# Gated linear attention followed by an MLP: from one head at a time through DRAM to one chunk of all heads at a time, interleaved with the MLP

## The chip, the core and the metric

The kernel runs on one core of one Trainium2 chip. The metric is device time in microseconds (us) of one launch, taken as the median of several runs. A core has five engines that run side by side, each in the order of its own instructions: TensorE (PE, matrix products and transposes; its weight loads are listed apart as PEld), VectorE (DVE), ScalarE (ACT, functions such as Exp, Ln and Silu, each from a table that has to be loaded), GpSimd (POOL) and SyncE (SP, which here only issues DMAs). Sixteen DMA engines move data between DRAM and on-chip memory; SP and POOL each have a queue of transfers that all sixteen serve. PE writes its results to PSUM, from where another engine has to fetch them.

## The reference

Attention has 4 batches, 8 heads, 768 steps and a head width of 48. Each head keeps a 48x48 state that decays by a gate per row and step. The MLP runs over the 3072 x 384 result, with a hidden width of 2048.

```
f = 1.0 / (1.0 + np.exp(-f_logit))
for t in range(S):
    state = f[:, :, t, :, None] * state + np.einsum('bhd,bhe->bhde', k[:, :, t], v[:, :, t])
    y[:, :, t] = np.einsum('bhd,bhde->bhe', q[:, :, t], state)
x = y.transpose(0, 2, 1, 3).reshape(B * S, H * D)
h = x @ w_in
out = (h * (1.0 / (1.0 + np.exp(-h)))) @ w_out
```

Both kernels use the chunked form of this: within a chunk of 128 steps, with `a` the running product of the gates, y is the lower triangle of (q·a)(k/a)ᵀ times v, plus (q·a) times the state before the chunk.

## The kernel before

**Attention** (L59 to L115) loops over the 4 batches, the 8 heads of each and the 6 chunks of each head: 192 passes. A head's four inputs are loaded by POOL with a cast to bf16 (L64 to L72) and its log gates are made by Sigmoid and Ln on ACT. A pass sums the log gates (`cs_ps`, L80), transposes q and k on PE (L82, L84), takes `a` = Exp (L86), `ia` by DVE's reciprocal (L88), makes `qg`, `ki` and `kb` on DVE (L91 to L95), transposes `kb` back (L97, L99), forms and masks the scores (`at_ps`, `atm`, L101, L103), the output (`y_ps`, L105, L106) and the next state (`d_ps`, `new_state`, L108, L110). The output, 128 rows of 48 floats, goes to a DRAM tensor called `bridge` (L115). Matmuls have 48 rows, or 48 columns, on one side or the other.

**The MLP** comes after that. Both weights are loaded by POOL (L120, L122) once attention's pools are closed. The 24 blocks of 128 tokens are read back from `bridge` (L140) and transposed on PE into `xT` (L143, L144). Then `h_ps` (L151) and Silu (L153) run over 16 blocks of the hidden width and 6 blocks of 512 tokens, and last `o_ps` (L158), its copy (L161) and the output (L162).

A scheduler in the framework sets each engine's order in this kernel: the loads of a next head, for example, stand ahead of the current one's passes, bounded by the two buffers of pool `hb`.

Of the kernel before, what the change touches and what calls it, by code (L numbers as in the profile page):

```python
# [10 lines left out]
F32 = mybir.dt.float32  # L11
BF16 = mybir.dt.bfloat16
AF = mybir.ActivationFunctionType
ALU = mybir.AluOpType


@with_exitstack
def kernel(
    ctx: ExitStack,
    tc: tile.TileContext,  # L20
    q: bass.AP,
    k: bass.AP,
    v: bass.AP,
    f_logit: bass.AP,
    moe_w_in: bass.AP,
    moe_w_out: bass.AP,
    out: bass.AP,
):
# [16 lines left out]
    maskU = singles.tile([C, C], F32)  # L45
    make_upper_triangular(nc, maskU, 1.0, diag=True)
    ident = singles.tile([C, C], BF16)
    make_identity(nc, ident)

    attn_ctx = ExitStack()  # L50
    sb = attn_ctx.enter_context(tc.tile_pool(name="sb", bufs=3))
    hb = attn_ctx.enter_context(tc.tile_pool(name="hb", bufs=2))
    ps = attn_ctx.enter_context(tc.tile_pool(name="ps", bufs=1, space=bass.MemoryType.PSUM))
    ps2 = attn_ctx.enter_context(tc.tile_pool(name="ps2", bufs=1, space=bass.MemoryType.PSUM))
    psA = attn_ctx.enter_context(tc.tile_pool(name="psA", bufs=1, space=bass.MemoryType.PSUM))
    psY = attn_ctx.enter_context(tc.tile_pool(name="psY", bufs=2, space=bass.MemoryType.PSUM))
    stp = attn_ctx.enter_context(tc.tile_pool(name="stp", bufs=2))

    for b in range(B):  # L59
        for h in range(H):  # L60
            state = stp.tile([D, D], BF16)
            nc.vector.memset(state, 0.0)
            logf_all = hb.tile([C, NCH, D], BF16)
            nc.gpsimd.dma_start(out=logf_all, in_=f_logit[b, h].rearrange("(c ci) d -> ci c d", ci=C))  # L64
            nc.scalar.activation(logf_all, logf_all, AF.Sigmoid)
            nc.scalar.activation(logf_all, logf_all, AF.Ln)  # L66
            q_all = hb.tile([C, NCH, D], BF16)
            nc.gpsimd.dma_start(out=q_all, in_=q[b, h].rearrange("(c ci) d -> ci c d", ci=C))
            k_all = hb.tile([C, NCH, D], BF16)
            nc.gpsimd.dma_start(out=k_all, in_=k[b, h].rearrange("(c ci) d -> ci c d", ci=C))  # L70
            v_all = hb.tile([C, NCH, D], BF16)
            nc.gpsimd.dma_start(out=v_all, in_=v[b, h].rearrange("(c ci) d -> ci c d", ci=C))  # L72
            for c in range(NCH):
                s0 = c * C
                logf_cd = logf_all[:, c, :]
                q_cd = q_all[:, c, :]
                k_cd = k_all[:, c, :]
                v_cd = v_all[:, c, :]
                cs_ps = ps.tile([D, C], F32)
                nc.tensor.matmul(cs_ps, logf_cd, triu)  # L80
                qT_ps = ps2.tile([D, C], BF16)
                nc.tensor.transpose(qT_ps, q_cd, ident)  # L82
                kT_ps = ps2.tile([D, C], BF16)
                nc.tensor.transpose(kT_ps, k_cd, ident)  # L84
                a = sb.tile([D, C], F32)
                nc.scalar.activation(a, cs_ps, AF.Exp)  # L86
                ia = sb.tile([D, C], F32)
                nc.vector.reciprocal(ia, a)  # L88
                cs_last = a[:, C - 1:C]
                qg = sb.tile([D, C], BF16)  # L90
                nc.vector.tensor_mul(qg, qT_ps, a)  # L91
                ki = sb.tile([D, C], BF16)
                nc.vector.tensor_mul(ki, kT_ps, ia)  # L93
                kb = sb.tile([D, C], BF16)
                nc.vector.tensor_scalar(kb, ki, cs_last, None, ALU.mult)  # L95
                kbT_ps = ps.tile([C, D], BF16)
                nc.tensor.transpose(kbT_ps, kb, ident[:D, :D])  # L97
                kbT = sb.tile([C, D], BF16)
                nc.scalar.copy(kbT, kbT_ps)  # L99
                at_ps = psA.tile([C, C], F32)  # L100
                nc.tensor.matmul(at_ps, ki, qg)  # L101
                atm = sb.tile([C, C], BF16)
                nc.vector.tensor_mul(atm, at_ps, maskU)  # L103
                y_ps = psY.tile([C, D], F32)
                nc.tensor.matmul(y_ps, atm, v_cd, start=True, stop=False)  # L105
                nc.tensor.matmul(y_ps, qg, state, start=False, stop=True)  # L106
                d_ps = ps.tile([D, D], F32)
                nc.tensor.matmul(d_ps, kbT, v_cd)  # L108
                new_state = stp.tile([D, D], BF16)
                nc.vector.scalar_tensor_tensor(new_state, state, cs_last, d_ps,  # L110
                                               ALU.mult, ALU.add)
                state = new_state
                y_sb = sb.tile([C, D], F32)
                nc.scalar.copy(y_sb, y_ps)  # L114
                nc.sync.dma_start(out=bridge[b * S + s0:b * S + s0 + C, h * D:h * D + D], in_=y_sb)  # L115
# [8 lines left out]
    MT = 512
    n_mt = NT // MT
    n_kt = d_model // 128
    n_nt = d_ff // 128
    n_dt = d_model // 128

    xpool = ctx.enter_context(tc.tile_pool(name="xpool", bufs=1))  # L130
    hpool = ctx.enter_context(tc.tile_pool(name="hpool", bufs=1))
    ptp = ctx.enter_context(tc.tile_pool(name="ptp", bufs=2, space=bass.MemoryType.PSUM))
    php = ctx.enter_context(tc.tile_pool(name="php", bufs=4, space=bass.MemoryType.PSUM))
    pop = ctx.enter_context(tc.tile_pool(name="pop", bufs=2, space=bass.MemoryType.PSUM))
    opool = ctx.enter_context(tc.tile_pool(name="opool", bufs=3))

    xT = xpool.tile([128, n_kt, NT], BF16)
    for mi in range(NT // 128):
        x_sb = opool.tile([128, d_model], BF16)
        nc.gpsimd.dma_start(out=x_sb, in_=bridge[mi * 128:(mi + 1) * 128, :])  # L140
        for ki in range(n_kt):
            xt_ps = ptp.tile([128, 128], BF16)
            nc.tensor.transpose(xt_ps, x_sb[:, ki * 128:(ki + 1) * 128], ident)  # L143
            nc.vector.tensor_copy(xT[:, ki, mi * 128:(mi + 1) * 128], xt_ps)  # L144

    hT = hpool.tile([128, n_nt, NT], BF16)
    for ni in range(n_nt):
        for mi in range(n_mt):
            h_ps = php.tile([128, MT], F32)
            for ki in range(n_kt):  # L150
                nc.tensor.matmul(h_ps, w_in_sb[:, ki, ni * 128:(ni + 1) * 128], xT[:, ki, mi * MT:(mi + 1) * MT],  # L151
                                 start=(ki == 0), stop=(ki == n_kt - 1))
            nc.scalar.activation(hT[:, ni, mi * MT:(mi + 1) * MT], h_ps, AF.Silu)  # L153

    for mi in range(NT // 128):
        o_ps = pop.tile([128, d_model], F32)
        for ni in range(n_nt):
            nc.tensor.matmul(o_ps, hT[:, ni, mi * 128:(mi + 1) * 128], w_out_sb[:, ni, :],  # L158
                             start=(ni == 0), stop=(ni == n_nt - 1))
        o_sb = opool.tile([128, d_model], F32)  # L160
        nc.vector.tensor_copy(o_sb, o_ps)  # L161
        nc.sync.dma_start(out=out[mi * 128:(mi + 1) * 128, :], in_=o_sb)  # L162


# [28 lines left out]
```

## Time and profile before

| what | value |
|---|---|
| median of 3 runs | 632.35 us (632.18 to 632.67) |
| profiled execution: its span, first to last instruction | 630.9 us |
| ACT_TABLE_LOAD at L86, L65, L66 | 61 + 32 + 32, 1.283 us each |
| first `h_ps` of the dense MLP (timeline) | 504.27 us |
| bytes read from and written to DRAM | 29.88 MB, 9.44 MB |

The page of a profile names groups of instructions by line, engine and operation, with what goes out of and into them, the count, the busy time and the mean ns of one; behind the second bar stands how long the engine was idle just before them, and what ended that. Slices are fortieths of the span, with the busy share in tenths.

### The profile page before, as it was taken

The numbers are of one execution on the slowest core, as the hardware profiler recorded it, in microseconds if no ns is written. First come the engines' busy times: TensorE is split into PE (matmuls) and PEld (weight loads), VectorE is DVE, ScalarE is ACT, GpSimd is POOL, SyncE is SP. The second block draws the span as 40 slices with busy tenths as digits, with TensorE's granted clock in tenths as the row PEclk, the third lists the DMA queues.
The fourth block names the chain that finished last, engine by engine and source line by source line (L and its number), as shares of the span: only waits on it lengthen the run. The fifth ranks groups of instructions, "written<-read, shape, count | busy, mean of one in ns | idle before, by whom it ended". The sixth has DMA issues, their size and how long they took to land.

```text
span 630.9 us, 8131 instructions
## 1 busy us (share of the span) xinstructions
PE 438.1 (69%) x2273; PEld 226.0 (36%) x2280; DVE 388.9 (62%) x1280; ACT 359.1 (57%) x862; POOL 121.4 (19%) x164
## 2 busy tenths in 40 slices
PE   1666666666666666676666666666724699999997
PEld 0333333333333333333333333333311244446664
DVE  1888887777888877888888778888822400002221
ACT  6666777656667777666677776666301189970000
POOL 5222222322222322222223222222032300000000
PEclk9999999999999999999999999999999999999999
DMA  7444445545444454544444545444088500002222
GB/s 37 30 32 29 35 32 36 50 30 35 31 31 34 30 40 29 35 31 31 32 32 32 37 30 34 30 32 30 14 141 128 66 0 1 0 1 76 75 76 76
DMA packets 137422, 24.93 MB, mean 40 GB/s; under 512 B 128800, under 2 KB 136992, under 8 KB 137376
## 3 DMA queue, kind: packets, MB, share of 16 engines
q0 software_dynamic: 106272, 14.95, 35.0%
q1 hardware_dynamic: 31104, 9.45, 6.2%
q8 instruction: 18, 0.29, 0.2%
q14 instruction: 28, 0.23, 0.1%
HBM read 29.88 MB, written 9.44 MB: 62 GB/s over the span
## 4 chain that ended last, share of the span: by engine, by line
PE 29%; issue 28%; DVE 20%; ACT 11%; DMA 6%; POOL 6%; POOLq 0%; ACTq 0%; DVEq 0%
DVE ia L88 11%; PE o_ps L158 10%; PE h_ps L151 10%; DMA x_sb<-bridge 5%; ACT L66 4%; DVE new_state L110 3%; ACT a L86 3%; ACT L86 2%; DVE kb L95 2%; PE y_ps L105 2%; PE kbT_ps L97 2%; PE cs_ps L80 2%; DVE atm L103 2%; PE y_ps L106 1%; POOL logf_all L64 1%
## 5 line engine op out<-in xcount | busy, mean ns | idle before, releaser
L88 DVE RECIPROCAL ia<-a 48x128 f32<-48x128 f32 x192 | 180.0, 938 | 39.9 <-ACT a L86 39.9
L99 ACT COPY kbT<-kbT_ps 128x48 bf16<-128x48 bf16 x192 | 37.1, 193 | 85.8 <-PE kbT_ps L97 85.5
L80 PE MATMUL cs_ps<-triu,logf_all 128*48 128x128 bf16 x192 | 51.3, 267 | 46.9 <-ACT a L86 46.8
L82 PE MATMUL qT_ps<-ident,q_all 128*48 128x128 bf16 x192 | 54.4, 283 | 42.1 <-DVE qg L91 36.1
L161 DVE COPY o_sb<-o_ps 128x384 f32<-128x384 f32 x24 | 13.4, 558 | 109.5 <-PE o_ps L158 109.5
L86 ACT ACT_TABLE_LOAD x61 | 78.3, 1283 | 1.1
L153 ACT ACTIVATE hT<-h_ps 128x512 bf16<-128x512 f32 x96 | 57.3, 597 | 32.8 <-PE h_ps L151 28.4
L108 PE MATMUL d_ps<-v_all,kbT 128*48 128x48 bf16 x192 | 44.9, 234 | 42.2 <-ACT kbT L99 42.1
L151 PE MATMUL h_ps<-xT,w_in_sb 128*128 128x512 bf16 x281 | 67.6, 398 | 9.0 <-DMA w_in_sb<-in_moe_w_in_dram 8.8
L86 ACT ACTIVATE a<-cs_ps 48x128 f32<-48x128 f32 x192 | 52.1, 271 | 37.9 <-DVE new_state L110 27.7
L158 PE MATMUL o_ps<-w_out_sb,hT 128*128 128x384 bf16 x384 | 63.0, 327 | 6.2 <-DMA w_out_sb<-in_moe_w_out_dram 6.2
L110 DVE SCALAR_TENSOR_TENSOR new_state<-new_state,a,d_ps 48x48 bf16<-48x48 bf16 x160 | 37.9, 237 | 41.3 <-PE d_ps L108 41.3
L97 PE MATMUL kbT_ps<-ident,kb 48*128 48x48 bf16 x192 | 41.9, 218 | 29.5 <-DVE atm L103 18.6
L103 DVE TENSOR_TENSOR atm<-at_ps,maskU 128x128 bf16<-128x128 f32 x192 | 56.2, 293 | 6.0 <-PE at_ps L101 1.7
L84 PE MATMUL kT_ps<-ident,k_all 128*48 128x128 bf16 x192 | 57.6, 300 | 0.5 <-DMA k_all<-in_k_dram 0.5
L101 PE MATMUL at_ps<-qg,ki 48*128 48x128 bf16 x192 | 54.6, 284 | 0.0
L64 POOL DMA_DIRECT2D logf_all<-in_f_logit_dram x32 | 26.4, 826 | 145.7 <-PE at_ps L101 124.5
L91 DVE TENSOR_TENSOR qg<-qT_ps,a 48x128 bf16<-48x128 bf16 x192 | 52.8, 275 | 0.0
L93 DVE TENSOR_TENSOR ki<-kT_ps,ia 48x128 bf16<-48x128 bf16 x192 | 52.6, 274 | 0.0
L95 DVE TENSOR_SCALAR kb<-ki,a 48x128 bf16<-48x128 bf16 x192 | 52.1, 271 | 0.1
L114 ACT COPY y_sb<-y_ps 128x48 f32<-128x48 f32 x192 | 37.0, 193 | 25.4 <-PE y_ps L106 24.1
L158 PEld LDWEIGHTS <-hT 128*128 128x128 bf16 x384 | 37.6, 98 | 31.8 <-issue 4.1
(38 smaller groups left out, 537.2 us busy)
## 6 DMA issues: line engine op xcount, KB each, us to landing
bridge<-y_sb SPq DMA_DIRECT2D x192, 24.0 KB, 1.7
out_dram<-o_sb SPq DMA_DIRECT2D x24, 192.0 KB, 1.9
logf_all<-in_f_logit_dram POOLq DMA_DIRECT2D x32, 72.0 KB, 2.9
q_all<-in_q_dram POOLq DMA_DIRECT2D x32, 72.0 KB, 3.0
k_all<-in_k_dram POOLq DMA_DIRECT2D x32, 72.0 KB, 3.2
v_all<-in_v_dram POOLq DMA_DIRECT2D x32, 72.0 KB, 2.9
x_sb<-bridge POOLq DMA_DIRECT2D x24, 96.0 KB, 2.6
w_in_sb<-in_moe_w_in_dram POOLq DMA_DIRECT2D x1, 1536.0 KB, 10.9
```

The lines of the kernel that those rows point to most:

```text
L80: nc.tensor.matmul(cs_ps, logf_cd, triu)
L84: nc.tensor.transpose(kT_ps, k_cd, ident)
L86: nc.scalar.activation(a, cs_ps, AF.Exp)
L88: nc.vector.reciprocal(ia, a)
L95: nc.vector.tensor_scalar(kb, ki, cs_last, None, ALU.mult)
L97: nc.tensor.transpose(kbT_ps, kb, ident[:D, :D])
L101: nc.tensor.matmul(at_ps, ki, qg)
L103: nc.vector.tensor_mul(atm, at_ps, maskU)
L110: nc.vector.scalar_tensor_tensor(new_state, state, cs_last, d_ps, ALU.mult, ALU.add)
L151: nc.tensor.matmul(h_ps, w_in_sb[:, ki, ni * 128:(ni + 1) * 128], xT[:, ki, mi * MT:(mi + 1) * MT], start=(ki == 0), stop=(ki == n_kt - 1))
L153: nc.scalar.activation(hT[:, ni, mi * MT:(mi + 1) * MT], h_ps, AF.Silu)
L158: nc.tensor.matmul(o_ps, hT[:, ni, mi * 128:(mi + 1) * 128], w_out_sb[:, ni, :], start=(ni == 0), stop=(ni == n_nt - 1))
```

## The change

The kernel is rewritten around chunks. A **group** g is one chunk of 128 steps of all 4 batches and 8 heads: 512 tokens. There are 6 groups, and for each of them:

- `load(g)` (SP): the four inputs in f32, one DMA each, of 128 steps by 32 heads in pieces of 48 floats; two buffers.
- `prep(g)`: `e` = Exp(−f) and `lf` = Ln(1 + e), two ACTIVATEs of 1536 elements a row; v is cast into `vp`, in which zeros stand around each head; then for each batch the running sums `cs` (one matmul of 384 columns), `a` and `ia` by two Exp, `qg` on DVE and `ki` on POOL. `al` is the decay over the whole chunk, by 16 matmuls of one column. Heads lie 64 elements apart, so that two make 128 rows.
- `attend(g)`: for each batch 8 transposes of head pairs and one copy `qk`; 8 score matmuls and two masked products `atm`; the outputs `y_ps`, which come out transposed (384 features by 128 tokens) and are copied to `xT`, the operand of the MLP; and the state `st`, held in SBUF with zero blocks for the other heads.
- `mlp_in(g)` and `mlp_out(g)`: the same MLP, on the 512 tokens of the group. Both weights are loaded at the start (POOL, behind six memsets of 2048 elements a row).

The order is written out by hand. `interleave` takes parts from its streams, by the numbers that they yield, so that each gets through at the same rate. After `prep(0)`, attend(0) runs with prep(1); then iteration g has mlp_in(g) with the first half of attend(g + 1), and mlp_out(g) with its second half and prep(g + 2). Transposes run one batch ahead of scores and two ahead of outputs. `bridge`, its reads and the 72 transposes of x are gone, and so is the reciprocal.

```diff
-    bridge = nc.dram_tensor("bridge", (NT, HD), F32, kind="Internal").ap()
...
+    acc = ctx.enter_context(tc.tile_pool(name="acc", bufs=3, space=PSUM))
+    tps = ctx.enter_context(tc.tile_pool(name="tps", bufs=1, space=PSUM))
+    aps = ctx.enter_context(tc.tile_pool(name="aps", bufs=1, space=PSUM))
+    hps = ctx.enter_context(tc.tile_pool(name="hps", bufs=2, space=PSUM))
...
+    def load(g):
+        tiles = {}
+        for name, src in (("f", f_logit), ("k", k), ("q", q), ("v", v)):
+            t = ld.tile([C, B, H, D], F32, name=f"{name}_ld", tag=f"{name}_ld")
+            nc.sync.dma_start(out=t.rearrange("p b h d -> p (b h) d"), in_=group_view(src, g))
...
+    def prep(g):
...
+        nc.scalar.activation(e, t["f"], AF.Exp, scale=-1.0)
+        nc.scalar.activation(lf[i][:, :, :, 0:D], e, AF.Ln, bias=1.0)
+        for b in range(B):
+            nc.gpsimd.tensor_copy(
+                vp[i][:, b, 128:].rearrange("p (h w) -> p h w", w=VW)[:, :, 0:D], t["v"][:, b])
+        yield 0.0
+        for b in range(B):
+            cs = acc.tile([C, H, D], F32, name="cs", tag="acc")
+            nc.tensor.matmul(cs, triu, lf[i][:, b, :, 0:D], start=True, stop=True)
+            a = wk.tile([C, H, D], F32, name="a")
+            nc.scalar.activation(a, cs, AF.Exp, scale=-1.0)
+            ia = wk.tile([C, H, D], F32, name="ia")
+            nc.scalar.activation(ia, cs, AF.Exp, scale=1.0)
+            nc.vector.tensor_mul(qg[i][:, b, :, 0:D], t["q"][:, b], a)
+            nc.gpsimd.tensor_mul(ki[i][:, b, :, 0:D], t["k"][:, b], ia)
+            yield 162.0
+        al_ps = acc.tile([C, B, NP], F32, name="al_ps", tag="acc")
+        for b in range(B):
+            for p in range(NP):
+                nc.tensor.matmul(al_ps[:, b, p:p + 1], lf[i][:, b, 2 * p:2 * p + 2, :], ones,
...
+        def transposes(b):
...
+            sb = wk.tile([128, 2, NP, C], BF16, name="qk")
+            nc.vector.tensor_copy(sb, t_ps)
...
+        def outputs(b):
...
+                for n, (l, r) in enumerate(terms):
+                    nc.tensor.matmul(y_ps[:, t, :], l, r, start=(n == 0), stop=(n == len(terms) - 1))
+            nc.vector.tensor_copy(x[:, :, b, :], y_ps)
...
+        for s in range(B + 2):
+            if s < B:
+                order.append((transposes, s, 560.0))
+            if 1 <= s <= B:
+                order.append((scores, s - 1, 450.0))
+            if s >= 2:
+                order.append((outputs, s - 2, 1100.0))
+                if g < NCH - 1:
+                    order.append((state, s - 2, 450.0))
...
+    with tc.manual_schedule():
+        for _ in prep(0):
+            pass
+        interleave((attend(0), ATT), (prep(1), PREP))
+        for g in range(NCH):
+            if g + 2 < NCH:
+                load(g + 2)
...
+            first = [(mlp_in(g), 16 * 650.0)]
+            if att is not None:
+                first.append((half(att, ATT / 2), ATT / 2))
+            interleave(*first)
+            second = [(mlp_out(g), 16 * 650.0)]
+            if att is not None:
+                second.append((att, ATT / 2))
+            if g + 2 < NCH:
+                second.append((prep(g + 2), PREP))
+            interleave(*second)
```

**The middle of an iteration, ACT.** Before, ACT's rows in attention mix a head's gate functions with the Exp and the copies of each pass (`kbT` and `y_sb` are copies of PE's results).

```order
L65 ACT_TABLE_LOAD
L65 ACTIVATE logf_all<-logf_all 128x288
L114 COPY y_sb<-y_ps 128x48
L86 ACT_TABLE_LOAD
L86 ACTIVATE a<-cs_ps 48x128
```

Of the change, the same engine from the end of prep(1) through mlp_in(0) (L243, Silu) into prep(2):

```order
L150 ACTIVATE al<-al_ps 128x16
L243 ACT_TABLE_LOAD
L243 ACTIVATE hT<-h_ps 128x512 x16
L127 ACT_TABLE_LOAD
L127 ACTIVATE e<-f_ld 128x1536
L128 ACT_TABLE_LOAD
L128 ACTIVATE lf_105<-e 128x32x48
L137 ACT_TABLE_LOAD
L137 ACTIVATE a<-cs 128x384
L139 ACTIVATE ia<-cs 128x384
```

The gate functions of a group now stand in one place, behind all 16 Silu of the iteration.

**The same place, PE.** Before, PE's rows at a pass's start and the pass's rest go through single heads:

```order
L80 LDWEIGHTS logf_all
L80 MATMUL cs_ps<-triu,logf_all 48x128
L105 LDWEIGHTS atm
L105 MATMUL y_ps<-v_all,atm 128x48
L106 LDWEIGHTS qg
L106 MATMUL y_ps<-new_state,qg 128x48
```

Of the change, where the second half of iteration 0 has begun (L198 is the last of batch 1's outputs, L250 mlp_out; four `o_ps` stand ahead of the outputs):

```order
L198 LDWEIGHTS vp_112
L198 MATMUL y_ps<-atm,vp_112 128x128
L135 LDWEIGHTS triu
L135 MATMUL cs<-lf_105,triu 128x384
L250 LDWEIGHTS hT
L250 MATMUL o_ps<-w_out_sb,hT 128x384
```

`cs`, which reads what ACT's Ln writes, stands ahead of all but four of the 64 `o_ps`.

**The start, DVE.** Before, DVE's rows are a chain for one pass after another:

```order
L88 RECIPROCAL ia<-a 48x128
L91 TENSOR_TENSOR qg<-qT_ps,a 48x128
L93 TENSOR_TENSOR ki<-kT_ps,ia 48x128
L88 RECIPROCAL ia<-a 48x128
L95 TENSOR_SCALAR kb<-ki,a 48x128
L103 TENSOR_TENSOR atm<-at_ps,maskU 128x128
```

Of the change, from prep(0) (`qg_107`) into attend(0), with `qg_108` of prep(1) between its steps:

```order
L140 TENSOR_TENSOR qg_107<-q_ld,a 128x8x48 x4
L171 COPY qk<-t_ps 128x1024
L140 TENSOR_TENSOR qg_108<-q_ld,a 128x8x48
L171 COPY qk<-t_ps 128x1024
L183 TENSOR_TENSOR atm<-a_ps,triu 128x512 x2
L140 TENSOR_TENSOR qg_108<-q_ld,a 128x8x48
```

A product of group 1, which reads `q_ld` of load(1), now stands ahead of most of attend(0).

More of the change, by code (lines that the diff above doesn't have):

```diff
@@ L55 @@
-    psA = attn_ctx.enter_context(tc.tile_pool(name="psA", bufs=1, space=bass.MemoryType.PSUM))
-    psY = attn_ctx.enter_context(tc.tile_pool(name="psY", bufs=2, space=bass.MemoryType.PSUM))
-    stp = attn_ctx.enter_context(tc.tile_pool(name="stp", bufs=2))
-    for b in range(B):
[L60 to L115, printed above, removed]
@@ L120 @@
+    st = [singles.tile([C, NP, HD], BF16, name=f"st{i}") for i in range(B)]
+    for i in range(2):
+        nc.gpsimd.memset(lf[i], 0.0)
+        nc.gpsimd.memset(qg[i], 0.0)
+        nc.gpsimd.memset(ki[i], 0.0)
+        nc.vector.memset(vp[i], 0.0)
+    for b in range(B):
+        nc.vector.memset(st[b], 0.0)
+    w_in_sb = singles.tile([128, KT, d_ff], BF16)
     nc.gpsimd.dma_start(out=w_in_sb, in_=moe_w_in.rearrange("(ko ki) n -> ki ko n", ki=128))
-    w_out_sb = wpool.tile([128, d_ff // 128, d_model], BF16)
+    w_out_sb = singles.tile([128, NT, d_model], BF16)
@@ L122 @@
     nc.gpsimd.dma_start(out=w_out_sb, in_=moe_w_out.rearrange("(ko ki) n -> ki ko n", ki=128))
[L124 to L162, printed above, removed]
+    load(1)
@@ new lines, with mlp_in @@
+    ATT = 4 * (560.0 + 450.0 + 1100.0 + 450.0)
+    hT = {}
+    def mlp_in(g):
+        hT[g] = hp.tile([128, NT, MT], BF16, name="hT")
+        for n in range(NT):
+            h_ps = hps.tile([128, MT], F32, name="h_ps", tag="h_ps")
+            for kk in range(KT):
+                nc.tensor.matmul(h_ps, w_in_sb[:, kk, n * 128:(n + 1) * 128],
+                                 xT[g][:, kk].rearrange("p b c -> p (b c)"),
+                                 start=(kk == 0), stop=(kk == KT - 1))
+            nc.scalar.activation(hT[g][:, n, :], h_ps, AF.Silu)
+            yield 650.0
@@ new lines, in mlp_out @@
+    def mlp_out(g):
+        for b in range(B):
+            o_ps = hps.tile([C, d_model], F32, name="o_ps", tag="h_ps")
+            for n in range(NT):
+                nc.tensor.matmul(o_ps, hT[g][:, n, b * C:(b + 1) * C], w_out_sb[:, n, :],
+                                 start=(n == 0), stop=(n == NT - 1))
+                if n % 4 == 3 and n < NT - 1:
+                    yield 650.0
+            o_sb = op.tile([C, d_model], F32, name="o_sb")
+            nc.vector.tensor_copy(o_sb, o_ps)
+            r0 = b * S + g * C
+            nc.sync.dma_start(out=out[r0:r0 + C, :], in_=o_sb)
+            yield 650.0
@@ new lines, in chain, with half @@
+    def chain(*gens):
+        for gen in gens:
+            yield from gen
+    with tc.manual_schedule():
[5 more added lines that the diff above has]
+                load(g + 2)
+            att = attend(g + 1) if g + 1 < NCH else None
+            def half(gen, budget):
+                spent = 0.0
+                while spent < budget:
+                    try:
+                        c = next(gen)
+                    except StopIteration:
+                        return
+                    spent += c
+                    yield c
+            first = [(mlp_in(g), 16 * 650.0)]
[8 more added lines that the diff above has]
+            interleave(*second)
```

118 lines of the change are left out of this document (104 added, 14 removed).

## The prediction

> **What bounds the kernel now.** I read the page first: its span, the engines' shares, the slices and the chain.
>
> ```profile
> span 630.9 us, 8131 instructions
> PE 438.1 (69%) x2273; PEld 226.0 (36%) x2280; DVE 388.9 (62%) x1280; ACT 359.1 (57%) x862; POOL 121.4 (19%) x164
> ...
> PE   1666666666666666676666666666724699999997
> ...
> DVE  1888887777888877888888778888822400002221
> ...
> PEclk9999999999999999999999999999999999999999
> ...
> PE 29%; issue 28%; DVE 20%; ACT 11%; DMA 6%; POOL 6%; POOLq 0%; ACTq 0%; DVEq 0%
> ```
>
> A slice is 15.8 us. Up to slice 29 (457 us) VectorE (DVE) is the fullest engine and TensorE (PE) stands at six tenths: attention. Then come three slices of hand-over, and from 504 us PE is full: the MLP. No engine is the bound over the whole span. The groups by line say what attention spends.
>
> ```profile
> L88 DVE RECIPROCAL ia<-a 48x128 f32<-48x128 f32 x192 | 180.0, 938 | 39.9 <-ACT a L86 39.9
> ...
> L86 ACT ACT_TABLE_LOAD x61 | 78.3, 1283 | 1.1
> ...
> L103 DVE TENSOR_TENSOR atm<-at_ps,maskU 128x128 bf16<-128x128 f32 x192 | 56.2, 293 | 6.0 <-PE at_ps L101 1.7
> ...
> L91 DVE TENSOR_TENSOR qg<-qT_ps,a 48x128 bf16<-48x128 bf16 x192 | 52.8, 275 | 0.0
> L93 DVE TENSOR_TENSOR ki<-kT_ps,ia 48x128 bf16<-48x128 bf16 x192 | 52.6, 274 | 0.0
> L95 DVE TENSOR_SCALAR kb<-ki,a 48x128 bf16<-48x128 bf16 x192 | 52.1, 271 | 0.1
> ...
> L110 DVE SCALAR_TENSOR_TENSOR new_state<-new_state,a,d_ps 48x48 bf16<-48x48 bf16 x160 | 37.9, 237 | 41.3 <-PE d_ps L108 41.3
> ```
>
> One chunk of one head costs DVE 0.938 + 0.293 + 0.275 + 0.274 + 0.271 + 0.237 = 2.29 us, and 457 us over 192 of them is 2.38 us. So attention runs at DVE's pace, with tiles of 48 rows or 128 columns. The timeline shows the rest.
>
> ```profile
> 473.06 1.06 PE L151 MATMUL h_ps<-xT,w_in_sb 128*128 128x512 bf16 x2 [8.78 <-DMA w_in_sb<-in_moe_w_in_dram]
> ...
> 504.27 8.06 PE L151 MATMUL h_ps<-xT,w_in_sb 128*128 128x512 bf16 x29
> 519.72 20.45 PE L151 MATMUL h_ps<-xT,w_in_sb 128*128 128x512 bf16 x92
> ```
>
> PE waits for the weights, which are asked for only after attention, and for rows coming back from DRAM; the dense MLP follows.
>
> **What goes.** All of L88 to L115: the per-head chain, the reciprocal (now a second Exp on ScalarE), 192 writes of the bridge and its 24 reads, and the wait for weights. Nothing of the 457 us remains as it was, so I price the new program from its matmuls up.
>
> **PE per iteration.** In the last row 92 matmuls of 512 columns take 20.45 us: 0.222 us each.
>
> ```profile
> L158 PE MATMUL o_ps<-w_out_sb,hT 128*128 128x384 bf16 x384 | 63.0, 327 | 6.2 <-DMA w_out_sb<-in_moe_w_out_dram 6.2
> ...
> 499.49 0.63 PE L151 MATMUL h_ps<-xT,w_in_sb 128*128 128x512 bf16 x1
> 499.92 0.31 PE L143 MATMUL xt_ps<-ident,x_sb 128*128 128x128 bf16 x1
> ...
> 500.45 0.42 PE L143 MATMUL xt_ps<-ident,x_sb 128*128 128x128 bf16 x2
> ```
>
> 384 columns take 63.0/384 = 0.164 us. For 128 columns only a slow stretch has a row: two in 0.42 against one in 0.31 start 0.11 us apart. In that stretch 512 columns start 0.43 apart (1.06 − 0.63), 1.94 times the dense 0.222, although the PEclk row is full throughout. So 128 columns cost 0.06 us at full pace, and 0.11 at most. An iteration is then 48 × 0.222 + 64 × 0.164 = 21.2 us of MLP; transposes, scores and outputs are (32 + 32 + 64) × 0.06 = 7.7; states 4 × (0.164 + 4 × 0.06) = 1.6; `cs` 4 × 0.164 = 0.7; `al` 16 × 0.06 = 1.0. Sum: 32.1 us.
>
> **What PE waits for in an iteration.** The largest wait is new. In the second half PE has `cs` of the next group after 4 `o_ps` and one batch of outputs, and queues everything else behind it. `cs` needs `lf`, which ScalarE (ACT) makes only behind the 16 Silu.
>
> ```profile
> L153 ACT ACTIVATE hT<-h_ps 128x512 bf16<-128x512 f32 x96 | 57.3, 597 | 32.8 <-PE h_ps L151 28.4
> ...
> L86 ACT ACTIVATE a<-cs_ps 48x128 f32<-48x128 f32 x192 | 52.1, 271 | 37.9 <-DVE new_state L110 27.7
> ...
> L66 ACT ACTIVATE logf_all<-logf_all 128x288 bf16<-128x288 bf16 x32 | 14.2, 443 | 0.4
> ...
> 4.73 0.44 ACT L65 ACTIVATE logf_all<-logf_all 128x288 bf16<-128x288 bf16 x1 [2.70 <-DMA logf_all<-in_f_logit_dram]
> 5.19 1.28 ACT L66 ACT_TABLE_LOAD   x1
> 6.48 0.44 ACT L66 ACTIVATE logf_all<-logf_all 128x288 bf16<-128x288 bf16 x1
> ```
>
> ACT's slope is (597 − 271)/384 = 0.85 ns per element, so 1536 elements take 0.443 + 1248 × 0.85 ns = 1.5 us. After PE's last `h_ps`: Silu 0.6 and a 0.2 hop, load 1.28, Exp 1.5, load 1.28, Ln 1.5, hop 0.2: 6.6 us. PE has 4 × 0.164 + 16 × 0.06 = 1.6 us until then: it waits **5.0 us**, with nothing behind it to do. The Trainium skill (ScalarE: Activation LUTs, What ACT_TABLE_LOAD costs) adds about 1.38 us of drain to each switch; by that the wait would be 2.8 us longer, 11 us over four iterations. The last rows show no drain: the load starts 0.02 us after one ACTIVATE and the next starts with its end. The measurement decides.
>
> ```profile
> L144 DVE COPY xT<-xt_ps 128x128 bf16<-128x128 bf16 x72 | 13.7, 221 | 33.4 <-PE xt_ps L143 33.2
> L161 DVE COPY o_sb<-o_ps 128x384 f32<-128x384 f32 x24 | 13.4, 558 | 109.5 <-PE o_ps L158 109.5
> ...
> 493.49 0.27 PE L143 MATMUL xt_ps<-ident,x_sb 128*128 128x128 bf16 x1 [0.21 <-DVE xT L144]
> ```
>
> DVE's slope is (558 − 221)/256 = 1.32 ns per element: the 1024-wide `qk` copy takes 1.4 us, the two 512-wide mask products 1.6, `xT` 0.56, two state products 0.86, `qg` 0.61, `o_sb` 0.56, together 5.6 us a batch and 22.4 an iteration, well below PE. As `t_ps` has one buffer, the second transposes wait for the first copy: 1.4 + 0.2 less 3 `h_ps` (0.67) = 0.9 us. Some 12 other hops of 0.2 us (last row) make 2.4, bounded by 0 and 6. After a gap of 8.8 us PE was slow; after one of 5.0 perhaps: 3 us at half pace lose 1.5, half of that is 0.75. Iteration: 32.1 + 5.0 + 0.9 + 2.4 + 0.75 = **41.2 us**, four times 164.6.
>
> **The loads and the start.** A load is now 4 tensors of 4096 pieces of 192 bytes, 256 pieces on each of 16 DMA engines, on SP's queue.
>
> ```profile
> q0 software_dynamic: 106272, 14.95, 35.0%
> q1 hardware_dynamic: 31104, 9.45, 6.2%
> ...
> 5.00:10.00 5.00, 0.74 (x3) 0.39 (x4) 0.00 (x0) 4.61 (x6) 3.73 (x5) 1.00 1.70 87
> 545.00:631.00 86.00, 81.96 (x473) 46.25 (x473) 13.39 (x24) 19.07 (x32) 0.00 (x0) 1.00 0.16 56
> ...
> bridge<-y_sb SPq DMA_DIRECT2D x192, 24.0 KB, 1.7
> out_dram<-o_sb SPq DMA_DIRECT2D x24, 192.0 KB, 1.9
> ...
> w_out_sb<-in_moe_w_out_dram POOLq DMA_DIRECT2D x1, 1536.0 KB, 17.9
> ```
>
> From below: SP's queue (q1) took 6.2% × 16 × 630.9 = 626 us, of which the output took 0.16 × 86 × 16 = 220; 406 us over 24,576 bridge pieces of the same 192 bytes is 16.5 ns, 4.2 us a tensor. The casting loads once ran at 87 GB/s of 96-byte writes, 906 a us, 4.5 us a tensor. From above: q0's mean packet, 35.0% × 16 × 630.9/106272 = 33 ns, 8.5 us. I take 5.0, near the rows of the same queue and size. DVE reaches its first `qg` of prep(1) right after the first `qk` copy of attend(0), and POOL needs the fourth tensor before any `ki`; `cs` buffers tie PE to both. So attend(0) ends only behind load(1), eight tensors and both weights (17.9) on the same engines: 2.2 + 40 + 18 = 60.2 us. Then POOL (4 casts and a product, 0.71 us each by the slope of the next rows, (305 − 99)/127 = 1.6 ns an element, between 0.41 by the memset's 0.8 and 2.8 by L88's 7.3) 3.6 us, DVE (one `qg`, one `qk`, two batches of mask products, three `xT`, two states) 8.6 us, and hops: 14 us. The MLP starts at **74.2**, with 1.5 more until PE is at full pace.
>
> ```profile
> masks.py:199 POOL TENSOR_SCALAR_AFFINE_SELECT ident<-ident 128x128 bf16<-128x128 bf16 x1 | 0.3, 305 | 0.0
> ...
> masks.py:65 POOL MEMSET triu<- 128x128 bf16 x1 | 0.2, 205 | 0.3 <-POOLq L177 0.3
> ...
> L177 POOL MEMSET const-float32-1.0<- 128x1 f32 x1 | 0.1, 99 | 0.0
> ...
> 626.74 0.33 PE L158 MATMUL o_ps<-w_out_sb,hT 128*128 128x384 bf16 x1
> ```
>
> Later loads start with an iteration: on SP they stand behind the four outputs of the group before, whose last waits for `o_sb`. `al` stands 32 us into it and needs the fourth tensor, casts, one `ki`, one Exp: 2.2 + 4 × 5.0 + 4.1 = 26 us. Hidden; from 6.5 us a tensor no longer. POOL's upper end would add 4 us an iteration; it lies in the range.
>
> **Sum.** Iteration 4 has no prep and no states: 21.2 + 7.7 + 0.9 + 1.4 = 31.2. Iteration 5 is MLP alone with two `h_ps` buffers, 0.17 us short each time (0.67 + 0.6 + two hops against 1.33 a pair): 21.2 + 2.7 = 23.9. From the last matmul to the end 630.9 − 627.1 = 3.8. So 74.2 + 1.5 + 164.6 + 31.2 + 23.9 + 3.8 = 299.2 of span. The median of the runs, 632.35, is 1.45 above the profiled span: **301 us**.
>
> **Rivals.** *Loads at 8.5 us a tensor.* Start 102.2; the fourth tensor is ready 40 us into iterations 1 to 3, 8 late: 102.2 + 1.5 + 41.2 + 3 × 49.2 + 31.2 + 23.9 + 5.25 = 353. For it stands q0's mean, against it q1's. *PE stays at the slow pace.* The Trainium skill (TensorE: Matmul & The Clock Gate, Part 1) says that an idle window of 3.4 us halves the clock and a busy one restores it; the trace agrees, with 0.43 us after 8.8 idle and 29 matmuls in 8.06 us before the dense pace. If the interleaved waits keep it slow: 32.1 × 1.94 + 8.3 = 70.6 an iteration, 58.4 the fifth: 74 + 282 + 58 + 25 + 5 = 445. Against it: PE has work for four fifths of the iteration, not six tenths. *The interleaving covers nothing*, and DVE's steps add to PE's: 59.5 an iteration, in all 392. Against it: scores and outputs are a batch apart in PE's order. *Slower than before:* SP's queue makes pieces one after the other. Bridge DMAs of 128 pieces land in 1.7 us; were that all piece-making, 4096 take 54 us, 24 tensors and what follows 1396. It loses from 22.6 us a tensor (24 × 22.6 + 90 = 632). Against it: output DMAs with 8 times the bytes in as many pieces take 0.2 us more, and no DMA of over 128 pieces ever stood on that queue.
>
> **How the numbers follow.** Forecast 0.64, slow loads 0.16, slow PE 0.08, no cover 0.08, slower 0.04. The low end takes 4.2 us a tensor, the weights hidden beside them as far as the busy share of 1.70 lets transfers overlap (start 2.2 + 33.6 + 14 = 49.8), and no waits in an iteration but Ln's and `t_ps`'s (38.0): 49.8 + 4 × 38.0 + 29.8 + 21.2 + 5.25 = 258; the high end is 353. 0.11 us for every 128-column matmul (6 us an iteration, 26 in four) or 4 us of POOL in each stay below it. Together 0.80. Slower by over 0.2% 0.04, within 0.2% (about what a measurement can tell from none) 0.01, faster 0.95.
>
> **What would show it.** `h_ps` starting near 74 us and not before the fourth tensor of load(1); a PE gap of 5 us before `cs`, released by ACT's Ln, in each of iterations 0 to 3; `o_ps` rows of 0.164 us; iterations of 41 us. A packet time on q1 above 26 ns or `h_ps` rows of 0.43 us would make me wrong.

## The result, and the profile after

The changed kernel takes **272.56 us** (median of 4 runs, 270.51 to 273.65) against 632.32 us (632.18 to 632.67): the ratio is 0.4306, with a 95% interval of 0.4289 to 0.4324. The forecast was 301 us with a range of 258 to 353. The profiled execution has a span of 270.6 us. Two of the four runs of the serial kernel further down were over 1.5% slower than its fastest and are left out of its time.

These are lines of the page of the changed kernel: span, engines, slices, DMA queues, costly groups and DMA issues.

```profile
span 270.6 us, 3905 instructions
PE 197.8 (73%) x1616; PEld 117.7 (44%) x1632; DVE 108.1 (40%) x191; ACT 125.3 (46%) x184; POOL 49.3 (18%) x64
...
PE   0120003567993999975999939999849999999995
...
DVE  7420020965243555432743434644327443720011
...
PEclk9999999995997799997999977999959999999999
DMA  9999999999000015991119980159920100011011
...
q1 hardware_dynamic: 102144, 23.60, 55.9%
...
L250 PE MATMUL o_ps<-w_out_sb,hT 128*128 128x384 bf16 x384 | 77.3, 348 | 0.0
...
L171 DVE COPY qk<-t_ps 128x1024 bf16<-128x1024 bf16 x24 | 16.6, 691 | 45.0 <-PE y_ps L198 38.0
...
v_ld<-in_v_dram SPq DMA_DIRECT2D x6, 768.0 KB, 11.2
```

A slice is now 6.8 us. For six slices PE is almost idle, and the DMA row is full for ten: the start. Then PE is mostly at nine tenths, with one dent in each of four iterations, and in slices with or behind a dent the PEclk row, which was full throughout before, falls to 5 or 7 (once also at the end of the start). `o_ps` cost 77.3/384 = 0.201 us a matmul on average, where it cost 0.164 before. Cutting the span where the first `h_ps` of each group starts gives the stages. The columns are the stretch, its length, busy time and instructions of PE, PEld, DVE, ACT and POOL, the granted clock, the DMA share and GB/s.

```profile
0.00:64.30 64.30, 16.12 (x161) 11.86 (x162) 25.21 (x38) 19.94 (x28) 25.93 (x32) 0.97 1.29 186
64.30:103.10 38.80, 33.70 (x278) 20.02 (x281) 16.85 (x33) 21.60 (x32) 5.83 (x8) 0.87 0.17 34
103.10:140.40 37.30, 32.24 (x279) 19.34 (x281) 16.98 (x33) 21.31 (x32) 5.83 (x8) 0.95 0.65 107
140.40:178.10 37.70, 32.64 (x279) 19.41 (x281) 17.05 (x33) 21.32 (x32) 5.90 (x8) 0.91 0.68 106
178.10:215.70 37.60, 32.54 (x278) 19.44 (x280) 16.94 (x33) 21.29 (x32) 5.83 (x8) 0.91 0.68 106
215.70:244.70 29.00, 28.15 (x240) 16.93 (x241) 12.30 (x21) 10.26 (x17) 0.00 (x0) 1.00 0.08 29
244.70:270.60 25.90, 22.42 (x112) 10.72 (x111) 2.79 (x5) 9.56 (x16) 0.00 (x0) 1.00 0.10 38
```

The reader sees 64.3 us of start (forecast 74.2), four iterations of 37.3 to 38.8 us (41.2, the first with 1.5 more of slow pace), a fifth of 29.0 (31.2), and 25.9 for the last with the end (23.9 + 3.8). Of the iterations, only those with a prep have a clock below 1.00. Who waits for whom on PE, longest first (total us, times, longest):

```profile
PE cs L135 <- ACT lf L128: 35.3, 6, 11.3
PE t_ps L169 <- POOL ki L141: 21.5, 1, 21.5
PE t_ps L169 <- DVE qk L171: 3.0, 1, 3.0
PE a_ps L179 <- DVE atm L183: 3.0, 3, 2.2
```

`cs` waits for Ln six times; the wait for `ki` at the start is for data. This is the middle of iteration 1 on ACT, in the timeline (start, length, and in brackets idle time before and its releaser):

```profile
118.44 0.60 ACT L243 ACTIVATE hT<-h_ps 128x512 bf16<-128x512 f32 x1 [0.49 <-PE h_ps L240]
119.06 1.28 ACT L127 ACT_TABLE_LOAD   x1
120.35 1.48 ACT L127 ACTIVATE e<-f_ld 128x1536 f32<-128x1536 f32 x1
121.85 1.28 ACT L128 ACT_TABLE_LOAD   x1
123.15 1.48 ACT L128 ACTIVATE lf<-e 128x1536 bf16<-128x1536 f32 x1
```

and what PE does right behind it:

```profile
124.68 0.32 PE L135 MATMUL cs<-lf,triu 128*128 128x384 bf16 x1 [4.73 <-ACT lf L128]
124.84 2.32 PE L250 MATMUL o_ps<-w_out_sb,hT 128*128 128x384 bf16 x8
126.95 0.53 PE L135 MATMUL cs<-lf,triu 128*128 128x384 bf16 x1
```

The chain is the one of the forecast, step for step, and the gap is 4.73 us. Behind it 8 `o_ps` occupy PE for 2.1 us here and for 2.56 us in iterations 0, 2 and 3, where 1.3 would do.

### The profile page after: what moved, and what is told of

Read it like the earlier page. It is cut to its first block, busy times and chain, and to the rows that moved or that the text cites. A ratio compares the mean times of both kernels' runs of the same rounds, so it can differ in the third digit from the quotient of the medians.

```text
span 270.6 us, 3905 instructions
## 1 busy us (share of the span) xinstructions
PE 197.8 (73%) x1616; PEld 117.7 (44%) x1632; DVE 108.1 (40%) x191; ACT 125.3 (46%) x184; POOL 49.3 (18%) x64
## 4 chain that ended last, share of the span: by engine, by line
PE 64%; SPq 15%; ACT 9%; DMA 4%; DVE 4%; issue 1%; POOL 1%; POOLq 0%
PE o_ps L250 25%; PE h_ps L240 23%; SPq L74 15%; PE y_ps L198 6%; DMA v_ld<-in_v_dram 4%; PE t_ps L169 4%; PE a_ps L179 2%; ACT lf L128 2%; ACT e L127 2%; ACT L128 2%; ACT L127 2%; PE cs L135 2%; DVE atm L183 1%; DVE qk L171 1%; PE d_ps L206 1%
## 5 line engine op out<-in xcount | busy, mean ns | idle before, releaser
L243 ACT ACTIVATE hT<-h_ps 128x512 bf16<-128x512 f32 x96 | 57.3, 597 | 45.7 <-PE h_ps L240 43.8
L250 PE MATMUL o_ps<-w_out_sb,hT 128*128 128x384 bf16 x384 | 77.3, 348 | 0.0
L250 PEld LDWEIGHTS <-hT 128*128 128x128 bf16 x384 | 37.3, 103 | 44.4 <-issue 26.4
L140 DVE TENSOR_TENSOR qg<-q_ld,a 128x384 bf16<-128x384 f32 x24 | 15.1, 632 | 60.3 <-ACT a L137 48.3
L240 PEld LDWEIGHTS <-w_in_sb 128*128 128x128 bf16 x288 | 25.8, 98 | 27.5 <-issue 5.9
L171 DVE COPY qk<-t_ps 128x1024 bf16<-128x1024 bf16 x24 | 16.6, 691 | 45.0 <-PE y_ps L198 38.0
L183 DVE TENSOR_TENSOR atm<-a_ps,triu 128x512 bf16<-128x512 f32 x48 | 30.8, 684 | 4.9 <-PE a_ps L179 4.7
L141 POOL TENSOR_TENSOR ki<-k_ld,ia 128x384 bf16<-128x384 f32 x24 | 24.3, 1022 | 33.5 <-ACT ia L139 33.5
L198 PE MATMUL y_ps<-atm,vp 128*128 128x128 bf16 x240 | 23.5, 231 | 1.2 <-DVE xT L199 1.1
L213 DVE TENSOR_TENSOR st<-d_ps,al 48x192 bf16<-48x192 f32 x40 | 14.1, 353 | 14.1 <-PE d_ps L209 13.8
L198 PEld LDWEIGHTS <-vp 128*128 128x128 bf16 x240 | 17.6, 104 | 1.8 <-issue 1.6
L198 PE MATMUL y_ps<-qk,st 128*128 128x128 bf16 x120 | 16.5, 219 | 0.0
## 6 DMA issues: line engine op xcount, KB each, us to landing
w_in_sb<-in_moe_w_in_dram POOLq DMA_DIRECT2D x1, 1536.0 KB, 11.6
```

What stands on the lines that cost most here:

```text
L140: nc.vector.tensor_mul(qg[i][:, b, :, 0:D], t["q"][:, b], a)
L141: nc.gpsimd.tensor_mul(ki[i][:, b, :, 0:D], t["k"][:, b], ia)
L171: nc.vector.tensor_copy(sb, t_ps)
L183: nc.vector.tensor_mul(sb[:, r], a_ps[:, r], triu[:, None, :].to_broadcast([C, NP, C]))
L198: nc.tensor.matmul(y_ps[:, t, :], l, r, start=(n == 0), stop=(n == len(terms) - 1))
L213: nc.vector.tensor_mul(blocks[lo:lo + D, :, r * D:(r + 1) * D], d_ps[lo:lo + D, :, r * D:(r + 1) * D], alast[g][lo:lo + D, b, :, None].to_ ...
```

## The experiments

All of them are edits of the changed kernel, except two (named `b`) of the kernel before; where one builds on an earlier run, the text says so. "First `h_ps`" is where the start ends.

**The gap at `cs`: its removal.** `gates` holds Exp and Ln; f is loaded one iteration earlier (three dots stand for lines that are not shown).

```diff
     def prep(g):
...
-        nc.scalar.activation(e, t["f"], AF.Exp, scale=-1.0)
-        nc.scalar.activation(lf[i][:, :, :, 0:D], e, AF.Ln, bias=1.0)
...
         alast[g] = al
+        if g + 1 < NCH:
+            gates(g + 1)
         yield 0.0
...
-                load(g + 2)
+                load(g + 2, "kqv")
+            if g + 3 < NCH:
+                load(g + 3, "f")
```

> Exp and Ln of a group's gates are moved from behind the Silu of its iteration to the end of the prep before (f is loaded one iteration earlier, and once more at the start). Theory: the 4.7 us gap at cs, and about 2.4 us of slow TensorE behind it, are paid in each of iterations 0 to 3; iterations 1 to 3 fall from 37.5 to 30 to 31 us, the first keeps part of it because the gates of group 2 now stand ahead of its Silu; 272.5 falls to 244 to 252 us. Rival: the next wait (ki behind the fourth tensor and the casts, held by the three acc buffers) takes its place, iterations stay above 35 us and the time above 262.

Measured: 260.94 us (259.56 to 261.95); iterations 0 to 3 took 35.7, 35.1, 33.8 and 33.8 us. Between the two expectations: the gap at `cs` is gone from the iterations, but TensorE has a new wait, as its waits and its timeline in iteration 2 show.

```profile
PE h_ps L246 <- ACT hT L249: 10.6, 4, 2.9
...
141.17 1.02 PE L246 MATMUL h_ps<-xT,w_in_sb 128*128 128x512 bf16 x4 [2.86 <-ACT hT L249]
```

Ln now ends behind the iteration's last work, and Silu with it comes 4 to 5 us late; with two `h_ps` buffers PE stops. That was a reading, so the next run put Exp and Ln where ACT had been idle, between the last `ia` and `al` (the edit is shown against the run before):

```diff
+        if g + 1 < NCH:
+            gates(g + 1)
         al_ps = acc.tile([C, B, NP], F32, name="al_ps", tag="acc")
...
         alast[g] = al
-        if g + 1 < NCH:
-            gates(g + 1)
         yield 0.0
```

> As in the run with the gates early, but Exp and Ln of the next group's gates stand between the last a and ia of a prep and its al, where ScalarE was idle for 7 us, instead of behind al. Theory: the early gates gave back part of their gain because Ln ended 4 to 5 us into the next iteration and TensorE waited for Silu (10.6 us in four waits); with that gone iterations 1 to 3 take 31 to 32 us instead of 34 to 35 and the time is 249 to 255 us. Rival: the acc buffers hold TensorE instead (al later), iterations stay at 34 and the time at 258 to 262.

Measured: **246.15 us** (245.78 to 247.06), better than expected; iterations of 31.9, 31.4, 30.8 and 30.8 us. Its stage of iteration 2:

```profile
127.50:158.40 30.90, 30.57 (x280) 18.70 (x281) 17.62 (x33) 21.29 (x32) 5.89 (x8) 1.00 0.82 128
```

PE is busy for 30.57 of 30.90 us, with the clock at 1.00. So 30.8 us is what PE's own work takes in an iteration, and the gap with its consequences cost 26.4 us in all. `al`, the three `acc` buffers, POOL's casts and the loads hold nothing up at that pace.

**The half pace behind the gap.** Here the gap stays, but matmuls that nothing reads fill it.

```diff
+        if g >= 2:
+            junk = acc.tile([128, d_model], F32, name="junk", tag="acc")
+            for _ in range(26):
+                nc.tensor.matmul(junk, w_in_sb[:, 0, 0:128], w_out_sb[:, 0, :], start=True, stop=True)
         yield 0.0
```

> 26 matmuls of 384 columns, whose result nothing reads, stand ahead of cs in the preps of groups 2 to 5, in the time in which TensorE waits for Ln (26 x 0.162 = 4.2 us). Theory: the half pace behind the gap comes from the gap; with it filled cs and the o_ps behind it run at 0.162 us and each of iterations 0 to 3 loses about 2.3 us: 262 to 265 us. Rival: the pace falls for another reason (or the added work is itself late): 272 to 276 us.

Measured: 265.06 us (264.81 to 265.37); the iterations are 37.0, then 35.6 us. Its timeline and its stage of iteration 1:

```profile
118.26 4.39 PE L135 MATMUL junk<-w_out_sb,w_in_sb 128*128 128x384 bf16 x26
123.15 0.32 PE L139 MATMUL cs<-lf,triu 128*128 128x384 bf16 x1 [0.51 <-ACT lf L128]
123.31 1.46 PE L254 MATMUL o_ps<-w_out_sb,hT 128*128 128x384 bf16 x8
...
101.50:137.20 35.70, 34.86 (x306) 21.30 (x307) 18.09 (x33) 21.29 (x32) 6.11 (x8) 1.00 0.72 112
```

104 more matmuls make the kernel 7.5 us faster. `cs` starts no earlier relative to Ln; 8 `o_ps` start 0.162 us apart (0.32 in iterations 0, 2 and 3 with the gap), and the clock stays at 1.00. The half pace is a consequence of the gap and costs about 1.9 us an iteration (7.5 over four). The Trainium skill (TensorE: Matmul & The Clock Gate, Part 1) has this rule, an idle window of 3.4 us halving the clock. This case agrees: the stage of iteration 1 has a mean clock of 0.95 with the gap of 4.73 us, and of 1.00 with the gap filled.

**The start: the order of transfers.** First the weights were moved behind prep(0) on POOL's queue.

```diff
-    nc.gpsimd.dma_start(out=w_in_sb, in_=moe_w_in.rearrange("(ko ki) n -> ki ko n", ki=128))
-    nc.gpsimd.dma_start(out=w_out_sb, in_=moe_w_out.rearrange("(ko ki) n -> ki ko n", ki=128))
...
         for _ in prep(0):
             pass
+        nc.gpsimd.dma_start(out=w_in_sb, in_=moe_w_in.rearrange("(ko ki) n -> ki ko n", ki=128))
+        nc.gpsimd.dma_start(out=w_out_sb, in_=moe_w_out.rearrange("(ko ki) n -> ki ko n", ki=128))
         interleave((attend(0), ATT), (prep(1), PREP))
```

> Both weight loads are issued by POOL behind prep(0) instead of ahead of it. Theory: the start is set by transfers, and v of group 0 waited 18 us behind the weights; prep(0) ends near 24 us instead of 39 and the first h_ps starts at 54 to 60 us instead of 64.3: 262 to 268 us. Rival: the 16 DMA engines have the same work before the MLP in either order, and w_in as the last of it holds the first h_ps at 64: 271 to 274 us.

Measured: 273.7 us (272.85 to 274.58), first `h_ps` at 65.3: my theory fell. The rival's time came, but not by its reason: PE's first `h_ps` waits for `xT`, not for `w_in`. v of group 0 did come earlier (its casts start at 19.6 us instead of 35.2), but v of group 1, by POOL's timeline (changed kernel first, then this one), did not:

```profile
52.09 2.18 POOL L130 CAST vp<-v_ld 128x384 bf16<-128x384 f32 x4 [10.86 <-DMA v_ld<-in_v_dram]
```

```profile
53.49 1.85 POOL L128 CAST vp<-v_ld 128x384 bf16<-128x384 f32 x4 [25.81 <-DMA v_ld<-in_v_dram]
```

So the landing that counts might be that of the *eighth* tensor, with the weights still ahead of it. The next run put the weights behind it (the two lines stand after the casts of v in prep, for g = 1).

> Both weight loads are issued by POOL behind the casts of v of group 1, so that all eight tensors of load(0) and load(1) pass ahead of them. Theory: with the weights moved only behind prep(0) they still went ahead of the last three tensors of load(1), whose fourth landed near 53 us as before, and that landing, not the weights, holds attend(0) and the MLP behind it; now it lands near 36 us, attend(0) ends near 50, w_in is there by 52: the first h_ps starts at 50 to 54 us instead of 64.3, 259 to 263 us. Rival: transfers before the MLP are one sum in any order (w_in last, beside load(2)): first h_ps at 60 us or later, 268 to 274 us.

Measured: 261.01 us (260.33 to 261.84), first `h_ps` at 52.4. POOL's casts of group 1 and PE's first `h_ps`:

```profile
36.62 2.19 POOL L128 CAST vp<-v_ld 128x384 bf16<-128x384 f32 x4 [10.86 <-DMA v_ld<-in_v_dram]
...
52.42 0.61 PE L241 MATMUL h_ps<-xT,w_in_sb 128*128 128x512 bf16 x1 [0.76 <-DMA w_in_sb<-in_moe_w_in_dram]
```

The eighth tensor held the start of the changed kernel: it lands 15.5 us earlier, and the MLP starts 11.9 us earlier. Not all of the gain arrives: the first `h_ps` now waits 0.76 us for `w_in`, which is asked for behind all eight tensors; where the other 2.8 us went was not followed.

**What sets the pace of a load.** SP's issues of 4.15 us each could be cause or consequence. This run builds on the one before: its weights, too, stand behind the casts of v of group 1.

```diff
-            nc.sync.dma_start(out=t.rearrange("p b h d -> p (b h) d"), in_=group_view(src, g))
+            eng = nc.scalar if g < 2 and name in "kv" else nc.sync
+            eng.dma_start(out=t.rearrange("p b h d -> p (b h) d"), in_=group_view(src, g))
```

> The kernel with the weights behind the casts of v of group 1; k and v of load(0) and load(1) are issued by ScalarE's queue, f and q by SP's as before. Theory: SP's 4.15 us an issue is back pressure, the 16 DMA engines need 4.2 us for the 4096 pieces of a tensor whoever issues them; the eight tensors together still land near 36 us (the last cast of group 1 no earlier than 35) and the rate stays at 185 to 205 GB/s. Rival: the queue that makes the pieces is the bound; two queues bring the eight tensors in 20 to 25 us and the rate above 250 GB/s.

Measured: 265.33 us (one run), last casts at 38.5 us. The rate of its first slices:

```profile
GB/s 140 187 186 187 186 186 199 205 182 200 63 0 10 53 75 202 173 95 30 60 101 187 187 39 30 62 157 187 166 2 62 58 3 2 4 88 30 0 59 62
```

187 GB/s, as with one queue. The sixteen engines need 4.2 us for 4096 pieces of 192 bytes (36.6, less 0.7 until the first issue and an estimated 2 for the last landing, over eight), and SP's issue time is back pressure. Against 261.01 us with one queue this run loses 4 us, all of it before the first `h_ps` (57.1 against 52.4). The likely reason is ACT, which issues until 25 us and starts its first Exp only then.

**Interleaving undone.**

```diff
-            first = [(mlp_in(g), 16 * 650.0)]
...
+            for _ in mlp_in(g):
+                pass
+            for _ in mlp_out(g):
+                pass
+            if g + 2 < NCH and att is not None:
+                interleave((att, ATT), (prep(g + 2), PREP))
```

> The same parts without interleaving of the MLP: an iteration runs mlp_in, mlp_out, then attend of the next group with prep of the one after. Theory: the interleaving covers most of the waits between TensorE and VectorE; alone, attend and prep take 17 to 24 us beside 21 of MLP, partly at half pace, an iteration 40 to 46: 285 to 315 us. Rival: what the order covers is small, because the gap behind Ln is the only real wait and attention alone covers it as well: 268 to 278 us.

Measured: 290.7 us (289.87 and 291.51), iterations of 41.0 us (the fourth 39.4) and 36.3 for the fifth. PE's waits move to DVE; behind them stands the stage of iteration 2:

```profile
PE a_ps L179 <- DVE atm L183: 17.7, 17, 2.3
PE cs L135 <- ACT lf L128: 16.5, 2, 11.4
PE t_ps L169 <- DVE qk L171: 8.1, 12, 3.0
...
146.40:187.40 41.00, 35.35 (x281) 20.73 (x280) 17.62 (x33) 21.34 (x32) 5.88 (x8) 0.92 0.58 95
```

The waits for Ln are gone from the iterations, since ACT now runs Exp and Ln under `mlp_out`, and those for `atm` and `qk` have come. PE is also busy for 35.35 us at a clock of 0.92, against 30.57 at 1.00 without waits: a part of it runs at half pace. So the interleaving gains 18.1 us net, and paid for it with the gap that it made itself.

**The reciprocal, back in the new kernel and out of the old one.** In both the one line that makes `ia` changes:

```diff
-            nc.scalar.activation(ia, cs, AF.Exp, scale=1.0)
+            nc.vector.reciprocal(ia, a)
```

> The changed kernel with ia made by VectorE's reciprocal of a again, 384 columns, four times an iteration. Theory: the reciprocal costs about 2.8 us each, 11 us of VectorE in an iteration in which it was busy for 17 of 37.5; ki on POOL and with it ia's chain come later by 2 to 3 us, part of it on the path: 275 to 290 us. Rival: VectorE has room and nothing waits for it: 272 to 275 us.

Measured: 305.47 us (304.31 to 306.69): +33 us, more than expected, although DVE is busy for only 54% of the span. Part of its DVE timeline in iteration 1, and its PE wait that is new:

```profile
144.48 0.71 DVE L213 TENSOR_TENSOR st<-d_ps,al 48x192 bf16<-48x192 f32 x2
145.22 2.55 DVE L139 RECIPROCAL ia<-a 128x384 f32<-128x384 f32 x1
147.69 0.50 DVE L140 TENSOR_TENSOR qg<-q_ld,a 128x384 bf16<-128x384 f32 x1
148.20 1.29 DVE L183 TENSOR_TENSOR atm<-a_ps,triu 128x512 bf16<-128x512 f32 x2
...
PE y_ps L198 <- DVE xT L199: 17.5, 5, 4.2
```

Four reciprocals of 2.55 us stand in the second half ahead of `atm` and `xT`, for which PE waits; iterations are 44.4 us (the first 45.8), with a mean clock of 0.85 in iteration 2. The start has them too: the first `h_ps` stands at 69.0 us instead of 64.3.

```diff
-                nc.vector.reciprocal(ia, a)
+                nc.scalar.activation(ia, cs_ps, AF.Exp, scale=-1.0)
```

> The kernel before, with ia made by a second Exp on ScalarE (scale -1) from cs_ps instead of VectorE's reciprocal; nothing else. Theory: attention ran at VectorE's 2.29 us a pass, of which 0.94 were the reciprocal; with 1.35 left ScalarE is next at about 1.9 us a pass with its table loads, attention falls by 60 to 95 us: 540 to 575 us. Rival: a pass is a chain through all engines and single buffers, VectorE being only full, not the bound: 600 us or more.

Measured: 592.83 us (592.32 to 593.56), between theory and rival: −40 us. DVE falls to 40% of the span. PE's longest wait and ACT's share:

```profile
PE 427.6 (72%) x2273; PEld 225.8 (38%) x2280; DVE 238.9 (40%) x1088; ACT 392.1 (66%) x1055; POOL 121.5 (21%) x164
...
PE cs_ps L80 <- ACT ia L88: 80.1, 33, 3.4
...
102.08 1.28 ACT L66 ACT_TABLE_LOAD   x1
103.38 0.44 ACT L66 ACTIVATE logf_all<-logf_all 128x288 bf16<-128x288 bf16 x1
103.84 1.28 ACT L86 ACT_TABLE_LOAD   x1
...
105.61 0.27 PE L80 MATMUL cs_ps<-triu,logf_all 128*48 128x128 bf16 x1 [2.46 <-ACT ia L88]
```

150 us of DVE time are worth 40. PE's longest wait is for ACT, and it comes about once a head (33 waits, 32 heads), 2.46 us nearly each time: the single `cs_ps` buffer is held while ACT makes the Ln of the next head, with a table load on either side, ahead of `a` and `ia`.

**The kernel before with its weights early** (loaded at the third head instead of behind attention):

> The kernel before, with both weight loads issued inside attention, at the third head; nothing else. Theory: TensorE's waits for the weights at 473 and 480 us (8.8 and 6.2 us) go, less what reading the bridge back still holds: 617 to 622 us. Rival: the bridge's reads, which PE transposes between those waits, hold the same time: 628 to 633 us.

Measured: 625.44 us (624.34 to 626.06), between the two, 7 to 8 us faster. The waits for the weights are gone from PE's list: from the last `new_state` to the dense MLP it takes 33.3 us, where it took 46.9. But attention ends 6.1 us later, because early on ACT waits for the gates of a head whose load stands behind the weights:

```profile
28.64 0.44 ACT L70 ACTIVATE logf_all<-logf_all 128x288 bf16<-128x288 bf16 x1 [6.12 <-DMA logf_all<-in_f_logit_dram]
```

So 13 to 14 of the 15 us of waits were on the path, and the early transfer gave 6.1 of them back; reading the bridge back holds little.

**The two useful edits together:** Exp and Ln in the middle of a prep, weights behind the eighth tensor.

> The gates in the middle of a prep and the weights behind the casts of v of group 1, together. Theory: the two gains lie in different stretches (iterations 0 to 3, and the start) and add: first h_ps near 52, iterations of 31 to 32, 232 to 238 us. Rival: with the start shorter load(2) and the weights, which now run beside it, come too late for the shorter iteration 0, which keeps 5 us or more: 239 to 246 us.

Measured: **234.71 us** (234.25 to 235.18), a ratio of 0.3704 (0.3696 to 0.3712) to the kernel before, and the fastest of all versions. First `h_ps` at 52.6 us, iterations of 32.3, 31.4, 30.8 and 30.8. The gains add: 26.4 and 11.6 us alone, 37.9 together. Start and iteration 2 of it:

```profile
0.00:52.60 52.60, 16.86 (x160) 12.23 (x160) 26.79 (x39) 25.99 (x32) 25.63 (x32) 1.00 1.32 185
116.40:147.20 30.80, 30.63 (x282) 18.65 (x280) 17.53 (x33) 21.19 (x32) 5.89 (x8) 1.00 0.83 129
```

## Why the prediction was right

**The structure held.** A start bound by eight tensors and two weights, four iterations with one gap behind Ln, one without, one of MLP alone, and the end: each stands in the stage table. The 28.6 us between forecast span and measured span are sizes of terms: 9.9 in the start, 14.7 in the four iterations with the slow pace ahead of them, 2.2 in the fifth, 1.8 in the last with the end. Nearly all were taken too high. The slow pace behind the gap was taken too low, by about 1.1 us an iteration; that these 4 to 5 us made up for part of the others is luck.

No run takes the grouping by chunk itself apart. That the wide tiles bring most of the 360 us is read from the busy times (PE 438.1 to 197.8 us, DVE 388.9 to 108.1) and not tested.

- **The start**, 74.2 forecast, 64.3 measured; the slow pace that follows it was put at 1.5 us and cost about 1.1 (iteration 0 takes 31.9 us where the later ones take 30.8, with no gap). I took 5.0 us a tensor between bounds of 4.2 and 8.5; it is 4.2, the value of the same queue's packets, and saves 6.4 us. With the weights ahead of it the eighth tensor landed 15.5 us later than without (52.1 against 36.6), where 18 were taken. The stretch behind it took 12.2 us, not 14. The 2.2 us of lead had no row behind it; without the weights ahead, eight tensors of 4.2 leave 3.0 of the 36.6. That the eighth tensor holds the start was argued, and the two moves of the weights show it.
- **PE per iteration**, 32.1 forecast, 30.8 measured where nothing waits. The cost of 128 columns was right: 16 outputs take 0.89 us, 0.056 each. `al` and the 48-row scores were cheaper, at 0.026 and 0.041 us a matmul.
- **The gap behind Ln**, 5.0 forecast, 4.73 measured, and by its cause: with it gone the iteration is 30.8 us. The table loads have no drain behind them, at 1.28 us each with 0.01 or 0.02 us around. That is where I let the trace decide against the Trainium skill (ScalarE: Activation LUTs, What ACT_TABLE_LOAD costs).
- **The other waits**, 0.9 and 2.4 forecast, are about 0.3 together. The slope for `qk` was wrong: a 1024-wide bf16 copy takes 0.69 us, not 1.4, so `t_ps` is free almost in time; and the order hides the hops, as the serial version shows when it brings them back.
- **The slow pace behind the gap**, 0.75 forecast, about 1.9 measured. I gave it one chance in two; it came in every one of the four iterations.

37.5 us an iteration is then 30.8 + 4.7 + 1.9, to 0.1.

**The rivals.** Slow loads: no, 4.2 us a tensor. PE at the slow pace throughout: no, only after gaps. No cover: the serial kernel is the test, and at 291 us even that is far from 392. I had added DVE's 22.4 us to PE's, while DVE's real 17 us also overlap within attention. SP making pieces one by one: refuted by the two queues.

**What I read wrongly about the kernel before.** "Attention runs at DVE's pace" was half the truth. The sum of 2.29 us out of 2.38 fits, but without the reciprocal a pass takes only 0.2 us less, not 0.9, and once a head PE then waits 2.46 us for ACT and its table loads. The forecast did not rest on this, as it priced the new program from its matmuls up.

## What to carry to other kernels

When a program is rebuilt, price it from the new order: put the bounding engine's work in a row and ask at each place which other engine's chain must have ended by then. A long chain on a second engine (here Silu, two table loads, Exp, Ln) that is started only when the first one needs its result shows as one gap per iteration, and moving it into that engine's idle time bought 26 us. At the start, ask which transfer is awaited last, and move everything that is not needed until later behind *that* one; moving it behind an earlier one bought nothing, and a large transfer put early holds up the small ones behind it, as in the kernel before.

## What the runs showed that I had not expected

- A gap of 4.7 us on TensorE costs 2 us more, because the matmuls behind it run at half pace; useless matmuls in the gap make the kernel 7.5 us faster. With the early gates a gap of 2.86 us slowed PE in iteration 1 (6 `h_ps` in 2.65 us) and the same gap in iteration 2 did not (6 in 1.39).
- In the kernel before, the record of the granted clock stays at 1.00 throughout, although its matmuls of 512 columns started 0.43 us apart until 507 us; in the changed kernel it shows the half pace. In the fastest version, too, 8 transposes take 0.86 us at the head of iteration 0 and 0.45 a little later, under a record of 1.00. A full PEclk row is no proof of the full pace, and the distance of equal matmuls is.
- DVE copies 1024 bf16 elements out of PSUM in 0.69 us, as long as a 512-wide f32 product from there (0.684).
- Two issuing queues move pieces of 192 bytes no faster than one: 187 GB/s either way (one run with two queues).
- A reciprocal of 384 columns takes 2.55 us on DVE, 6.6 ns an element, and at 54% load it still cost 33 us by where it stood.
